# Casts of single heads and half copies for the first batch of an attention and max-out kernel

## Chip, cores and metric

The kernel runs on one core of one Trainium2 chip. The metric is the device time of one execution in microseconds; several executions give a median. A profile of one execution shows every instruction with its engine, line and tile. The engines are TensorE (PE in the profile, its weight loads PEld), VectorE (DVE), ScalarE (ACT), GpSimd (POOL) and SyncE (SP, which here only issues transfers).

## What is computed

Attention over 4 batches, 8 heads, 768 positions of 64 numbers, followed by a max-out layer. Heads marked in `is_retrieval` (three of eight) attend to all earlier positions, the others to a window of 64 and the first 4 positions:

```python
scores = scale * np.matmul(q, k.transpose(0, 1, 3, 2))
stream_keep = causal & (is_sink | in_win)
mask = np.where(retr[0, :, 0, 0, None, None], full_mask, stream_mask)
scores = np.where(mask[None, :, :, :], scores, -1000000000.0)
a = np.exp(scores - max) / sum
x = (a @ v), heads side by side: 3072 rows of 512
h1 = x @ w1          # 512 -> 1024
h2 = x @ w2
out = np.maximum(h1, h2) @ w_out     # 1024 -> 512
```

(The softmax and the reshaping are shortened here.)

## The kernel before

Everything is computed on TensorE in bfloat16. The max-out is rewritten: with wd = w1 - w2 and wm = w2 @ w_out, the result is relu(x @ wd) @ w_out + x @ wm. So, before the dense layers, w1 and w2 are subtracted (L442), w2 is cast, turned on TensorE (L453) and copied, and multiplied with w_out (L464).

Heads are taken in pairs, four pairs in a batch, sixteen in all (`pair`, L659). The heads are permuted so that the three that attend to everything come first: pair 0 of a batch has two such heads, pair 1 one, pairs 2 and 3 none. For each pair, q, k and v are loaded head by head into buffers `ld` (nine of them, three for a pair), cast to bfloat16 into `qb` (L681 to L685), turned by six 128x128 transposes into one bank of PSUM (L690 to L695), and copied from there to `qk` (L696). One bank holds the 768 bfloat16 columns of q or of k, and the copy rearranges them. For batch 0 the first half of the positions of v comes with three transfers at the start; only the late half is loaded by pair.

`attend` (L522) then computes scores into PSUM (L579), in batch 0 adds the mask by matmuls with an identity (L587), takes the exponential on ScalarE (L600), multiplies with v (L624) and divides by the sums on VectorE (L640, L643). When a batch's four pairs are done its result is turned (L739) and goes through the dense layers (L757, L781, L788), which run among the attention of the next batches.

No engine's order is written by hand. Each piece of work is an `Op` with a cost for every engine that may do it, the operations and buffers that it needs, and a priority. `Plan.schedule` (L74) is a list scheduler: over and over it takes, for each engine, the operation that can start first by its own model (of those that can start at once, the one of lowest priority), and of these the one with the earliest start, then the earliest end. The order that comes out is the order in which instructions are issued on each engine, which works through its queue in that order. Plan time 0 lies near 4.2 us of the trace, where the first planned matmul starts. Waits between engines are put in by the framework.

Points of the model that matter here. Transfers are served one after the other, each at its own rate (L140), from a first moment set by `DMA_FIRST` and `EARLY` (L78). SP takes the startable transfer of lowest priority: the loads of pair r have r, r + 0.01 and r + 0.02 for q, k and v, and the twelve quarters of the weights have the priorities of `LATER` (L176). One quarter of w_out is loaded ahead of the plan (`EARLY`) and is taken as landed at a fixed planned time (L433). VectorE and GpSimd take turns at a port for operations marked `shared` (L114 to L117): one may not start while the other's is under way. `warm` (L417) runs 42 matmuls on TensorE at the start.

Of the kernel before, what the change touches and what calls it, by code (L numbers as in the profile page):

```python
# [10 lines left out]
BF16 = mybir.dt.bfloat16  # L11
I32 = mybir.dt.int32
ALU = mybir.AluOpType
ACT = mybir.ActivationFunctionType
# [156 lines left out]
DMA_FIRST = -2.2  # L171
# [1 line left out]
WIDE_PAIRS = (1, 1, 1, 1, 1, 1, 1, 1, 1, 0, 0, 0, 0, 0, 0, 0)  # L173
X_XBAR = (0, 1, 1, 1)
EARLY = (('wo', 3),)
LATER = {('w2', 0): 3.93, ('w2', 1): 3.55, ('w2', 2): 3.4, ('w2', 3): 3.03, ('w1', 0): 5.86, ('w1', 1): 4.21, ('w1', 2): 6.83, ('w1', 3): 6.11, ('wo', 0): 3.53, ('wo', 1): 1.32, ('wo', 2): 0.84, ('wo', 3): 0.93}  # L176
MASK_TO = 1
NORM = 0.80
PO_TWO = 2
# [1 line left out]
WARM = 4.6  # L181
# [7 lines left out]
def kernel(  # L189
# [19 lines left out]
    nc = tc.nc  # L209
    V = nc.vector  # L210
    B, H, S, D = q.shape
# [28 lines left out]
    ident = tl("ident", [128, 128])  # L240
# [56 lines left out]
    def copy(e, o, i):  # L297
        if e == "ACT":
            nc.scalar.copy(out=o, in_=i)  # L299
        else:  # L300
            issued[e].append((V if e == "DVE" else nc.gpsimd).tensor_copy(out=o, in_=i).ins)  # L301
# [75 lines left out]
    def run(full, head, col, exact):  # L377
        P = Plan(*((SHIFT, HOLD) if exact else ({}, {})))
# [4 lines left out]
        sc_p, po_p, mm_p = map(Pool, map(list, (sc_t, po_t, mm_t) if PO_TWO or not exact else (sc_t, po_t[:1], po_t[1:] + mm_t)))  # L383

        c_m = None
        if exact:
            def f(e):
                V.tensor_sub(out=smk[:, 0:128], in0=causal[:, 0:128], in1=far0[:, 0:128])
                for i in (1, 2, 7, 8, 9):
                    V.tensor_sub(out=smk[:, 128 * i:128 * i + 128], in0=causal[:, 0:128], in1=far[:, 0:128])  # L390
                for i in (3, 4, 5, 6):
                    V.tensor_scalar(out=smk[:, 128 * i:128 * i + 128], in0=far0[:, 128:256], scalar1=-1.0, scalar2=1.0,
                                    op0=ALU.mult, op1=ALU.add)
                for m, o in ((tri, ntri), (smk, nsmk)):
                    V.tensor_scalar(out=o, in0=m, scalar1=1.0, scalar2=-NEG, op0=ALU.subtract, op1=ALU.mult)
            c_m = P.op(f, {"DVE": 2.6}, prio=-20)
        else:
            d_ir = P.op(lambda e: nc.sync.dma_start(out=ir, in_=ir_ap.rearrange("p (h t) -> p h t", t=2)),
                        {"SP": 0.5}, prio=-20, size=0.008, rate=0.3)

            def f(e):
                V.tensor_scalar(out=irn, in0=ir, scalar1=0.0, scalar2=float(H), op0=ALU.not_equal, op1=ALU.mult)
                V.tensor_tensor(out=flag, in0=irn[:, :, 0], in1=irn[:, :, 1], op=ALU.max)
                V.tensor_scalar(out=nsf, in0=flag, scalar1=1.0 / H, scalar2=-1.0, op0=ALU.mult, op1=ALU.add)
                V.tensor_scalar_mul(out=bias_j, in0=nsf, scalar1=-NEG)
                V.tensor_scalar_mul(out=bias_0, in0=bias_j, scalar1=nsink)
                for s in range(H):
                    for m in range(2):
                        V.scalar_tensor_tensor(
                            out=msk[:, s, m, :], in0=(far0 if m == 0 else far), scalar=nsf[:, s:s + 1],  # L410
                            in1=causal, op0=ALU.mult, op1=ALU.add)
            c_m = P.op(f, {"DVE": 5.0}, [d_ir], prio=-20)

        if exact:
            bk = Buf(mm_p)

            def warm(e, bk=bk):  # L417
                for _ in range(int(WARM / 0.107)):
                    nc.tensor.matmul(bk.t[:, 0, 0:128], lhsT=ident, rhs=ident, start=True, stop=True)
            P.op(warm, {"PE": WARM}, (), [bk], prio=-100)  # L420
        d_w = {}
        for name in ("w2", "w1", "wo"):
            for c in range(4):
                if (name, c) in EARLY:
                    P.number += 1
                else:
                    d_w[name, c] = P.op(lambda e, name=name, c=c: load_weight(name, c), {"SP": 0.5},
                                        prio=LATER[name, c], size=0.524, rate=0.35)

        def landed(*keys):  # L430

            return dict(deps=[d_w[k] for k in keys if k in d_w],
                        ready=max([0.0] + [DMA_FIRST + 6.05 + 1.7 * EARLY.index(k) for k in keys if k in EARLY]))  # L433
        wd_ops, w2_ops, wo_ops, wm_ops, w2t_ops = [], [], [], [], []
        for c in range(4):
            w2_ops.append(P.op(lambda e, c=c: copy(e, w2_bf[(slice(None),) + quarter(c)], w_raw[1][(slice(None),) + quarter(c)]),
# [10 lines left out]
        for fch in range(FC):  # L447
            bk = Buf(mm_p)
# [6 lines left out]
            o = P.op(tr, {"PE": 0.23}, w2_ops[2 * (fch // 4):2 * (fch // 4) + 2], [bk], prio=300 + fch)  # L455
            w2t_ops.append(P.op(lambda e, fch=fch, bk=bk: copy(e, w2t[:, fch, :], bk.t[:, 0].bitcast(BF16)[:, 0:d_model]),
                                {"DVE": 0.34, "ACT": 0.5}, [o] + wo_ops, [bk], prio=52 + fch))
        for c in range(KC):
            bk = Buf(mm_p)
# [196 lines left out]
        def tok(t):  # L656
            return t.rearrange("c (p n) -> c p n", n=NB)

        def pair(b, p):  # L659
            r = b * HP + p  # L660
            s0 = 2 * p
            if p == 0:
                xs[b], xt[b], xt_ops[b], norms[b] = Buf(xs_p), Buf(xt_p), [], ([], [])
            raws, loads = [], []
            for i, src in enumerate((q, k, v)):
                t = Buf(ld)
                raws.append(t)
                order, rate = ("(p n)", WIDE) if wide[r] and src is not v else ("(n p)", NARROW)
                two = []
                n0 = NB // 2 if b == 0 and src is v else 0  # L670
                for h in range(2):
                    two.append(P.op(lambda e, t=t, src=src, h=h, order=order, n0=n0: nc.sync.dma_start(
                        out=t.t[:, h, n0:], in_=src[b, bass.ds(head(s0 + h), 1), 128 * n0:].rearrange(
                            f"o {order} d -> p (o n) d", p=128)),
                        {"SP": 0.5}, (), [t], prio=r + 0.01 * i, size=0.0983 if n0 else 0.197, rate=rate))
                loads.append(two)
            qk, vb = Buf(qk_p), Buf(vb_p)
            tk, cast = [], []
            qb = Buf(qb_p)
            for i in range(2):  # L680
                def f(e, i=i):  # L681
                    for h in range(2):
                        copy(e, qb.t[:, i, :, h, :], raws[i].t[:, h])
                cast.append(P.op(f, {"POOL": 0.95, "DVE": 0.75} if b == 0 else {"POOL": 0.95}, loads[i],
                                 [raws[i], qb], prio=r + 0.01 * i, shared=True))  # L685
                if not wide[r]:
                    continue
                bk = Buf(mm_p)

                def tr(e, i=i, bk=bk):  # L690
                    psb = bk.t[:, 0].bitcast(BF16)
                    for n in range(NB):
                        nc.tensor.transpose(psb[:, n * 128:(n + 1) * 128],  # L693
                                            qb.t[:, i, n].rearrange("p h d -> p (h d)"), ident)
                o = P.op(tr, {"PE": 0.34}, [cast[i]], [qb, bk, qk], prio=90 + 2 * r)  # L695
                tk.append(P.op(lambda e, bk=bk, i=i: copy(  # L696
                    e, tok(qk.t[:, i]), bk.t[:, 0].bitcast(BF16)[:, 0:S].rearrange("c (n p) -> c p n", p=128)),
                               {"DVE": 0.90, "ACT": 0.7}, [o], [bk, qk], prio=r))
            if not wide[r]:
                tk.append(P.op(lambda e: nc.sync.dma_start_transpose(  # L700
                    out=qk.t.rearrange("c i (n p) -> c (i n) p", p=128),
                    in_=qb.t.rearrange("p i n h d -> p (i n h d)")),
                    {"SP": XBAR}, cast, [qb, qk], prio=r - 0.5, size=0.393, rate=0.2))
            n0 = NB // 2 if b == 0 else 0
            ov = []
            if b == 0:
                def fh(e):
                    for h in range(2):
                        copy(e, vb.t[:, h, 0:n0, 0:D], v_half[:, bass.ds(head(s0 + h), 1)].rearrange(
                            "p o (n d) -> p (o n) d", d=D))  # L710
                ov.append(P.op(fh, {"POOL": 0.6, "ACT": 0.6}, bufs=[v_held, vb], prio=r + 0.04, ready=DMA_FIRST + 5.2))

            def fv(e):
                for h in range(2):
                    copy(e, vb.t[:, h, n0:, 0:D], raws[2].t[:, h, n0:])
            ov.append(P.op(fv, {"POOL": 0.58, "DVE": 0.48} if b == 0 else {"POOL": 0.95}, loads[2],
                           [raws[2], vb], prio=r + 0.05, shared=True))

            last[0] = attend(b, p, qk, vb, tk, ov, r)
# [111 lines left out]
    with tc.If(match >= 1) as branch:  # L831
        _, at = nc.values_load_multi_w_load_instructions(
            perm[0:1, 0:H], engines=(mybir.EngineType.SP, mybir.EngineType.Pool, mybir.EngineType.Activation), min_val=0, max_val=H - 1,
            skip_runtime_bounds_check_because="a permutation of the heads")
# [45 lines left out]
```

## Time and profile before

| | us |
|---|---|
| median of 9 executions | 187.81 |
| lowest, highest | 186.58, 190.58 |
| the profiled execution | 188.12 |
| its span, first to last instruction | 186.3 |
| PE busy | 172.2 |
| ACT busy | 115.0 |
| DVE busy | 87.9 |
| POOL busy | 49.7 |

The mean granted clock of TensorE in the profiled execution was 0.972 of full speed. Busy times of engines overlap. A matmul's duration in the profile includes its way through the array, so TensorE shown as busy need not be working at its peak. "Idle before" in a row is the time that the engine stood before that instruction, with what ended the wait. A transfer's row on SP is its issue; it lands some microseconds later (a median of 4.8 for a load of q, 6.5 for a quarter of w1 or w2).

### The profile page before, as it was taken

The page shows a single profiled execution, that of the slowest core. Times are in us where ns is not written, and L with a number is a line of the kernel's source. Part 1 is how long each engine was busy: PE and PEld are TensorE (multiplying, and loading weights), DVE is VectorE, ACT ScalarE, POOL GpSimd, SP SyncE. Part 2 cuts the span into 40 slices and gives each one's busy share as a digit, 9 for nine tenths or more (in the row PEclk, how much of TensorE's full clock was granted, in tenths as well). Part 3 has the DMA queues.
Part 4 walks back from the last instruction along what each step waited for, and adds up shares of the span by engine and source line. Part 5 has one row for each costly group of instructions (what it writes and reads, how often), then busy time and mean ns, then how long its engine had stood idle before and what let it go on. Part 6 is the DMA issues. An engine that isn't in the chain of part 4 may idle for free.

```text
span 186.3 us, 4604 instructions
## 1 busy us (share of the span) xinstructions
PE 172.2 (92%) x1663; PEld 101.2 (54%) x1663; DVE 87.9 (47%) x247; ACT 115.0 (62%) x191; POOL 49.7 (27%) x107
## 2 busy tenths in 40 slices
PE   1848989899999999999999999999999999999990
PEld 1825665656666555555565556446555545545460
DVE  5636685868788386544478273354743000000000
ACT  3236699968889678726894478268845624426330
POOL 2101051356995765523125415200000000000000
PEclk9975699999999999999999999999999999999999
DMA  5999999999999998999999999994016612012032
GB/s 117 293 240 349 288 262 341 310 315 327 311 307 234 201 224 201 240 244 172 270 208 252 240 219 194 322 202 174 4 58 177 106 60 113 0 73 96 4 113 70
DMA packets 79553, 36.96 MB, mean 198 GB/s; under 512 B 68642, under 2 KB 73506, under 8 KB 79522
## 3 DMA queue, kind: packets, MB, share of 16 engines
q1 hardware_dynamic: 79522, 36.58, 79.0%
q8 instruction: 15, 0.25, 0.6%
q14 instruction: 16, 0.13, 0.2%
HBM read 25.17 MB, written 6.29 MB: 169 GB/s over the span
## 4 chain that ended last, share of the span: by engine, by line
PE 80%; DMA 8%; SPq 2%; DVE 2%; issue 1%; DVEq 0%; ACT 0%
PE mm L757 12%; PE mm L781 11%; PE po L624 8%; PE sc L579 8%; PE po L757 8%; PE po L781 7%; PE mm L788 6%; DMA raw<-in_moe_w_dram 5%; PE sc L781 4%; PE po L788 3%; DMA ld<-in_q_dram 3%; PE mm L464 3%; PE sc L757 2%; PE sc L788 2%; PE mm L693 2%; SPq L310 1%
## 5 line engine op out<-in xcount | busy, mean ns | idle before, releaser
L600 ACT ACTIVATE at_all<-sc 128x1024 bf16<-128x1024 f32 (+2 forms) x72 | 59.6, 870 | 8.2 <-PE sc L587 4.1
L757 PEld LDWEIGHTS <-wd_bf 128*128 128x128 bf16 x256 | 23.2, 98 | 14.0
L301 POOL CAST qb<-ld 128x384 bf16<-128x384 f32 x50 | 24.1, 507 | 19.5 <-DMA ld<-in_k_dram 8.1
L757 PE MATMUL mm<-xt,wd_bf 128*128 128x384 bf16 x140 | 27.6, 326 | 0.0
L624 PEld LDWEIGHTS <-at_all 128*128 128x128 bf16 x472 | 22.1, 100 | 9.5 <-issue 1.5
L624 PE MATMUL po<-vb,at_all 128*128 128x65 bf16 x472 | 26.8, 198 | 0.1
L579 PE MATMUL sc<-qk 64*128 64x128 bf16 (+2 forms) x364 | 23.6, 243 | 1.8 <-ACT qk L299 0.9
L643 DVE TENSOR_TENSOR xs<-po,rz 128x192 f32 x64 | 22.8, 357 | 3.1 <-DVE rz L640 0.9
L781 PEld LDWEIGHTS <-raw 128*128 128x128 bf16 x152 | 14.1, 98 | 13.6
L579 PEld LDWEIGHTS <-qk 64*128 64x128 bf16 x364 | 12.8, 95 | 14.5 <-issue 9.9
L301 POOL CAST vb<-ld 128x384 bf16<-128x384 f32 (+1 forms) x28 | 12.9, 484 | 24.4 <-DMA ld<-in_v_dram 10.4
L640 DVE RECIPROCAL rz<-po 128x6 f32<-128x6 f32 x32 | 6.2, 193 | 26.6 <-PE po L624 26.5
L757 PE MATMUL po<-xt,wd_bf 128*128 128x384 bf16 x88 | 17.9, 326 | 0.0
L781 PE MATMUL mm<-wo_bf,raw 128*128 128x512 bf16 x64 | 16.1, 379 | 0.0
L611 DVE TENSOR_TENSOR at_all<-at_all,smk 128x1024 bf16<-128x1024 bf16 (+3 forms) x27 | 15.2, 582 | 0.0
L788 PEld LDWEIGHTS <-xt 128*128 128x128 bf16 x100 | 9.3, 97 | 9.3
L611 DVE TENSOR_TENSOR at_all<-at_all,tri 128x256 bf16<-128x256 bf16 (+1 forms) x36 | 9.8, 305 | 6.4 <-ACT at_all L600 6.4
L788 PE MATMUL mm<-wm_bf,xt 128*128 128x512 bf16 x48 | 12.3, 379 | 0.0
L299 ACT COPY ot<-mm 128x512 f32<-128x512 f32 x9 | 5.3, 585 | 11.1 <-PE mm L788 10.6
L765 ACT ACTIVATE raw<-mm 128x384 bf16<-128x384 f32 x20 | 9.8, 490 | 2.9 <-PE mm L757 2.6
L781 PE MATMUL po<-wo_bf,raw 128*128 128x512 bf16 (+1 forms) x48 | 11.3, 361 | 0.0
L299 ACT COPY qk<-mm 128x768 bf16<-128x768 bf16 x9 | 7.3, 807 | 5.0 <-PE mm L693 4.4
(91 smaller groups left out, 189.7 us busy)
## 6 DMA issues: line engine op xcount, KB each, us to landing
ld<-in_q_dram SPq DMA_DIRECT2D x32, 192.0 KB, 4.8
ld<-in_k_dram SPq DMA_DIRECT2D x32, 192.0 KB, 4.6
out_dram<-ot SPq DMA_DIRECT2D x23, 256.0 KB, 2.6
ld<-in_v_dram SPq DMA_DIRECT2D x24, 192.0 KB, 4.1
raw<-in_moe_w_dram SPq DMA_DIRECT2D x8, 512.0 KB, 6.5
raw<-in_moe_w_out_dram SPq DMA_DIRECT2D x4, 512.0 KB, 6.0
xt<-in_v_dram SPq DMA_DIRECT2D x3, 256.0 KB, 3.6
ld<-in_v_dram SPq DMA_DIRECT2D x8, 96.0 KB, 3.9
```

The costliest lines, as they stand in the source:

```text
L299: nc.scalar.copy(out=o, in_=i)
L301: issued[e].append((V if e == "DVE" else nc.gpsimd).tensor_copy(out=o, in_=i).ins)
L579: nc.tensor.matmul(sc.t[:, k, off:off + w], lhsT=qk.t[64 * h:64 * h + 64, 1, j * 128:(j + 1) * 128], rhs=qk.t[64 * h:64 * h + 64, 0, q0:q0 ...
L600: nc.scalar.activation(out=a.t[:, k:k + m, 0:n], in_=sc.t[:, k:k + m, 0:n], func=ACT.Exp, scale=scale, bias=0.0 if bias is None else bias[ ...
L611: issued["DVE"].append(V.tensor_mul(out=y, in0=y, in1=z).ins)
L624: nc.tensor.matmul(po[u].t[:, 0, o:o + D + 1], lhsT=a.t[:, k, off + t * 128:off + (t + 1) * 128], rhs=vb.t[:, h, j, :], **fresh(u))
L640: V.reciprocal(out=rz_, in_=p4[:, :, :, D])
L643: V.tensor_tensor(out=xs[b].t[:, n0:n0 + nn, bass.ds(col(s0 + h), D)], in0=p4[:, i, :, 0:D], in1=rz_[:, i].unsqueeze(2).to_broadcast([128, ...
L757: nc.tensor.matmul(bk.t[:, 0, 0:GT], lhsT=wd_bf[:, c, f * 128:(f + 1) * 128], rhs=xt[b].t[:, g * NB // NG:(g + 1) * NB // NG, c, :], start ...
L765: nc.scalar.activation(out=gt.t[:, f, :], in_=bk.t[:, 0, 0:GT], func=ACT.Relu)
L781: nc.tensor.matmul(bk.t[:, 0, 0:m1 - m0], lhsT=gt.t[:, f, t * 128:(t + 1) * 128], rhs=wo_bf[:, f, m0:m1], start=(f == 0), stop=False)
L788: nc.tensor.matmul(bk.t[:, 0, 0:m1 - m0], lhsT=xt[b].t[:, c0 // 128, c, :], rhs=wm_bf[:, c, m0:m1], start=False, stop=(c == KC - 1))
```

## The change

For batch 0, the cast of q or k of a pair was one step with two instructions, one for each head, given to GpSimd or VectorE as a whole; it becomes two steps of one head each, which wait each for its own load and are placed one by one. The copy of the turned q or k out of PSUM was one step with one instruction on VectorE or ScalarE; for batch 0 it becomes two steps, each of half of the positions, which are placed one by one. With that come new numbers for the planner: other priorities of the weights' quarters, 0.55 in place of 0.5 for the issue of a load, and a planned landing 0.5 later for the early quarter of w_out. The definition of `warm` moves up in the text, in the same branch.

```diff
-LATER = {('w2', 0): 3.93, ('w2', 1): 3.55, ('w2', 2): 3.4, ('w2', 3): 3.03, ('w1', 0): 5.86, ('w1', 1): 4.21, ('w1', 2): 6.83, ('w1', 3): 6.11, ('wo', 0): 3.53, ('wo', 1): 1.32, ('wo', 2): 0.84, ('wo', 3): 0.93}
+LATER = {('w2', 0): 3.98, ('w2', 1): 3.71, ('w2', 2): 3.13, ('w2', 3): 0.06, ('w1', 0): 4.72, ('w1', 1): 5.94, ('w1', 2): 6.68, ('w1', 3): 7.85, ('wo', 0): 1.81, ('wo', 1): 3.16, ('wo', 2): 0.46, ('wo', 3): 1.9}
...
-                        ready=max([0.0] + [DMA_FIRST + 6.05 + 1.7 * EARLY.index(k) for k in keys if k in EARLY]))
+                        ready=max([0.0] + [DMA_FIRST + 6.55 + 1.7 * EARLY.index(k) for k in keys if k in EARLY]))
...
-                        {"SP": 0.5}, (), [t], prio=r + 0.01 * i, size=0.0983 if n0 else 0.197, rate=rate))
+                        {"SP": 0.55}, (), [t], prio=r + 0.01 * i, size=0.0983 if n0 else 0.197, rate=rate))
...
-                def f(e, i=i):
-                    for h in range(2):
-                        copy(e, qb.t[:, i, :, h, :], raws[i].t[:, h])
-                cast.append(P.op(f, {"POOL": 0.95, "DVE": 0.75} if b == 0 else {"POOL": 0.95}, loads[i],
-                                 [raws[i], qb], prio=r + 0.01 * i, shared=True))
+                one_ = []
+                for hs in ((0,), (1,)) if b == 0 else ((0, 1),):
+                    def f(e, i=i, hs=hs):
+                        for h in hs:
+                            copy(e, qb.t[:, i, :, h, :], raws[i].t[:, h])
+                    one_.append(P.op(f, {"POOL": 0.48, "DVE": 0.38} if b == 0 else {"POOL": 0.95},
+                                     [loads[i][h] for h in hs], [raws[i], qb], prio=r + 0.01 * i, shared=True))
+                cast += one_
...
-                o = P.op(tr, {"PE": 0.34}, [cast[i]], [qb, bk, qk], prio=90 + 2 * r)
-                tk.append(P.op(lambda e, bk=bk, i=i: copy(
-                    e, tok(qk.t[:, i]), bk.t[:, 0].bitcast(BF16)[:, 0:S].rearrange("c (n p) -> c p n", p=128)),
-                               {"DVE": 0.90, "ACT": 0.7}, [o], [bk, qk], prio=r))
+                o = P.op(tr, {"PE": 0.34}, one_, [qb, bk, qk], prio=90 + 2 * r)
+                for p0, p1 in ((0, 64), (64, 128)) if b == 0 else ((0, 128),):
+                    w = (p1 - p0) / 128
+                    tk.append(P.op(lambda e, bk=bk, i=i, p0=p0, p1=p1: copy(
+                        e, tok(qk.t[:, i])[:, p0:p1],
+                        bk.t[:, 0].bitcast(BF16)[:, 0:S].rearrange("c (n p) -> c p n", p=128)[:, p0:p1]),
+                                   {"DVE": 0.1 + 0.8 * w, "ACT": 0.1 + 0.65 * w}, [o], [bk, qk], prio=r))
```

## The prediction

> **What bounds the kernel now.** I read the page's engine shares and its 40 slices first, then the chain of waits over 0 to 50 us and over the rest, then the table of windows and the timeline of the first 40 us. The page gives TensorE 92% of the span. The chain says what stands ahead of that:
>
> ```profile
> 10.32 5.95 DMA ld<-in_q_dram
> ...
> 25.05 9.79 DMA raw<-in_moe_w_dram
> ...
> 34.86 0.70 DVE w_bf L301
> ...
> 37.65 0.86 PE mm L464 x4
> ...
> 49.76 0.21 DVE rz L640
> 49.97 0.02 issue
> 49.99 0.37 DVE xs L643
> ```
>
> Columns are start, duration, what. Until 34.8 us the chain goes from transfer to transfer. The last of them is the fourth quarter of w2, whose cast ends at 35.6. From there every step is TensorE's, but for one hole of about 1.05 us (49.74 to 50.79), until the output's tail at 181.6. So the end can move by three things only: when that quarter lands, how much TensorE work of batch 0 is still undone by 37.65, and holes after it. TensorE's own work is not touched: no matmul is added or removed.
>
> The windows by 5 us (span, then busy time and count of PE, PEld, DVE, ACT, POOL, then clock, DMA share, GB/s) show what batch 0 runs against:
>
> ```profile
> 10.00:15.00 5.00, 3.19 (x30) 1.79 (x31) 1.64 (x5) 2.58 (x3) 0.00 (x0) 0.69 0.96 268
> 15.00:20.00 5.00, 4.29 (x39) 2.65 (x39) 3.55 (x7) 3.05 (x4) 0.64 (x2) 0.50 1.09 340
> 20.00:25.00 5.00, 5.00 (x81) 3.81 (x80) 4.05 (x14) 3.58 (x7) 0.58 (x2) 0.79 0.92 236
> 25.00:30.00 5.00, 4.26 (x59) 2.71 (x56) 3.66 (x9) 4.84 (x8) 2.17 (x8) 1.00 0.97 336
> 30.00:35.00 5.00, 4.89 (x76) 3.17 (x72) 3.50 (x9) 4.96 (x8) 0.52 (x2) 1.00 1.01 339
> ```
>
> The DMA engines are full from 10 us on (shares 0.92 to 1.09), so w2's last quarter lands by the sum of the bytes ahead of it. ScalarE is the bound between 25 and 35 (9.80 of 10 us). TensorE runs at half clock in 15 to 20; in windows of 1 us that is so from 12 to 22.
>
> And the start, as the timeline has it:
>
> ```profile
> 11.01 0.36 DVE L301 CAST qb<-ld 128x384 bf16<-128x384 f32 x1 [0.28 <-DMA ld<-in_k_dram]
> 11.41 0.35 DVE L301 CAST vb<-ld 128x192 bf16<-128x192 f32 x1
> ...
> 11.98 0.80 ACT L299 COPY qk<-mm 128x768 bf16<-128x768 bf16 x1 [0.36 <-PE mm L693]
> ...
> 12.68 0.36 DVE L301 CAST vb<-ld 128x192 bf16<-128x192 f32 x1 [0.92 <-DMA ld<-in_v_dram]
> 12.83 0.13 PEld L579 LDWEIGHTS <-qk 64*128 64x128 bf16 x4 [1.06 <-ACT qk L299]
> ```
>
> The first scores wait for ScalarE's copy of k; VectorE is stuck in its queue until 12.68, on a cast of v.
>
> **The casts by single heads.** The instructions stay 16: before, one step issued two, now two steps issue one each. In the trace each cast already waits for its own head's load (the casts at 8.98, 9.85, 10.37, 11.01 are apart), so an earlier start is not won by the split. Whether they change engine I worked out by hand from the planner's rules, for the order only: at each cast of pair 0 VectorE and GpSimd could start at the same planned time (GpSimd may not start before VectorE's turn at the port has ended), and the tie goes to the lower cost, 0.38 against 0.48. So they stay on VectorE and the term is 0. If one goes to GpSimd it costs 0.50 instead of 0.36 (rows of 128x384), 0.14 on the path; if one really ran beside another it would win 0.36. Bounds for the start: -0.36 to +0.28 (q and k).
>
> **The copies in halves.** Eight copies become sixteen. The half (384 columns) is not in the trace as a copy; the nearest rows of that width out of PSUM are ScalarE's 128x384 activation, 0.49, and VectorE's 128x384 operation, 0.55 (L767). So a pair of halves takes 0.55 side by side and 1.04 in turn, against 0.80 on ScalarE alone. For the k of pair 0 neither end decides. By the planner's costs k's transposes are due at 7.46, when the cast of v's late heads (due 7.15, ending 7.63) is already placed on VectorE; ScalarE takes the first half, VectorE the second, behind that cast. In the trace that cast waits for its load until 12.68 and ends at 13.04. The second half then runs 13.05 to 13.60, and the scores start near 13.65 instead of 12.83: **+0.8**, where a clean split would have given 11.98 + 0.55 = 12.53, that is -0.3. I take +0.8, because the order is fixed in the queue and the load's time is not changed. Queued behind the waiting instruction on VectorE are only weight casts (their loads are later), so nobody else waits.
>
> The Trainium skill speaks against running the halves side by side at all: PSUM — Partial Sum Buffer, "PSUM bank collisions raise a hardware error", says that two engines, ScalarE and VectorE both reading included, must not be in one bank of the same partitions at once and are to be guarded by bank. Both halves lie in one bank (768 bf16 are 1,536 bytes). If the program is guarded that way, each pair costs 1.04 plus a semaphore, if not 0.55; no instruction of this trace shows such a pair.
>
> Later, where ScalarE is the bound, the copies of pairs 2 and 3 cost it 4 halves in place of 2 whole ones: 4 x 0.49 - 2 x 0.80 = **+0.36**. Ends: -1.6 (none of the eight halves on ScalarE) and +2.3 (all eight, 8 x 0.49 - 1.60); the planner takes whichever engine is free first, so four is the middle.
>
> **The order of loads.** SP issues by priority (pair r has r to r + 0.02, weights have LATER). Before: pair 0, wo2, pair 1, wo1, pairs 2 and 3, w2.3, w2.2, wo0, w2.1, w2.0, pair 4; the timeline of SP agrees. After: pair 0, w2.3, wo2, pair 1, wo0, pairs 2 and 3, w2.2, wo1, w2.1, w2.0, pair 4. The set ahead of w2.0 is the same, so its landing at 34.8 is costed at 0 (bounds ±0.5, about a tenth of a share over the 5 us from 20, where the engines were at 0.92, and as much the other way). w1's quarters change places among themselves; its last stays ahead of pair 7, whose buffers are not yet free when SP gets there: 0. But pairs 1 and 2 each come one chunk later: 524 KB at (268 + 340)/2 = 304 GB/s is 1.72 us.
>
> For pair 1 that reads: q's second head landed at 16.27 (the chain), its transposes followed at 16.71, ahead of the score of pair 0's fourth tile (17.68), which stood behind them in TensorE's queue. The first exponential of pair 1 came 6.50 after the landing, at 22.77. After: landing 17.99; planned one tile later, the transposes now stand behind that score, whose 0.54 + 0.33 (chain) is done in the wait. 17.99 + 6.50 - 0.87 = 23.62, **+0.85** on pair 1, in which the late start above is contained, since pair 0's tiles have that much room (ScalarE stood 1.56 us before the exponential at 18.65). Ends: +0.35 if the halves run side by side and TensorE is never blocked, +1.72 if the order does not adapt. Pair 2's casts stood ready behind other work (22.57, no wait), so its delay is hidden up to about 1.2 us (22.57 less the landing near 21.4: k's issue at 16.8 and 4.6 to landing); 0.5 is left, behind pair 1's delay: 0.
>
> The gain: w2.3's cast leaves the stretch after 22 us (0.69 on VectorE at 28.42). VectorE is not the bound there (7.2 of 10), ScalarE is, and it has w2.2's cast of 1.04 at 30.34. If the planner now gives that to VectorE, -1.04, else 0. I take half, **-0.52**.
>
> The half clock: TensorE got its full clock back at 22, after working without a hole from 17. If the work that ends there comes 0.85 later, that much more time passes at half speed: 0.5 x 0.85 = **+0.42**; ends 0 and +1.7 (a further third of that 10 us stretch, 3.4 us, at half rate). The skill's TensorE: Matmul & The Clock Gate, Part 1, has the clock decided in free-running windows of about 3.4 us, idle ones halving it; the 10 us at half clock here would be three such windows. By that rule the cost would be either 0 or about 1.7, nothing between.
>
> **Sum.** 0 + 0.36 + 0.85 - 0.52 + 0.42 = +1.11 at the end of batch 0's attention. It doesn't all reach the end: from 37.65 on TensorE has the combined weight's product (8 x 0.86 = 6.9 us) to do meanwhile. What of batch 0 is still open then must be done later. TensorE was busy throughout 20 to 25, so I let 0.9 of it through (ends: none and all): **+1.0**. The profiled execution took 188.12 (span 186.3 and 1.82 around it), 0.31 above the median of 187.81; on it the sum gives 189.1, on the median **188.8**. Own range of this case: 187.9 to 189.8.
>
> About 0.5% (0.94 us) is what a measurement of this kernel can tell from no change.
>
> **Rivals.**
> 1. *Weights earlier win* (0.30). For: w2.3 takes the place of wo2, cast at 15.23, in the queue and can be cast some 13 us earlier than at 28.42; if with that w2.2's cast leaves ScalarE, it ends batch 0 before 35.6, so its matmuls that now stand in the chain behind it (0.35 at 36.49 and 0.19 at 37.46) are gone from there, and the hole of 1.05 at 49.74 is closed by the new order: -1.59, 186.2. Against: the last quarter's landing sets the product's start and has not moved.
> 2. *The clock comes back a step later* (0.15). One mechanism: TensorE waits for pair 1's q and k between 18 and 22 us, the full clock comes at 25.5 instead of 22, and 3.4 us of work take twice as long: +1.7 in place of 0.42, with the rest of the sum let through whole: 1.11 - 0.42 + 1.7 = 2.4, 190.2. It decides from a hole of about 1 us there (before: none).
> 3. *Nothing comes through* (0.13, 187.8). The product at 37.65 and what follows hide all of it, and the casts stay where they were; for it speaks that TensorE is the whole chain from there.
> The forecast itself has 0.42; it lies on the edge of what can be told apart, and 0.30 of its 0.42 above it, because its ends upward are larger.
>
> **Chances.** Slower: 0.30 + 0.15 + 0.02 (of rival 3) = 0.47. Faster: 0.28 (of rival 1) + 0.01 + 0.03 = 0.32. Within: 0.11 + 0.02 + 0.08 = 0.21. The range goes from just below rival 1's time, 185.8, to just above rival 2's, 190.4; about 0.12 and 0.06 lie outside.
>
> **What would show it.** Right: a copy of 128x384 on VectorE starting after the cast of v at about 13.0, the first scores near 13.6, pair 1's first exponential after 23.2, both halves' rows near 0.49 and 0.55, w2.0 landing at 34.8, all casts of pair 0 on VectorE. Wrong: the first scores before 12.6; w2's last cast before 34; the product's start (first L464) earlier than 37; a clock of 1.00 already before 21. The full clock first after 24 would be rival 2.

## The result, and the profile after

| | before | after |
|---|---|---|
| median, us | 188.29 (54 executions) | 190.25 (17) |
| lowest, highest | 186.58, 190.58 | 188.99, 192.24 |
| the profiled execution | 188.12 | 189.86 |
| its span | 186.3 | 187.7 |
| clock over the span | 0.972 | 0.990 |

The ratio is 1.0119 with a 95% interval of 1.0092 to 1.0146; it leaves out the executions of either kernel that ran in a slower state, so it isn't the quotient of the two medians above. That is slower by about 2.2 us (0.0119 x 188.29). The forecast was slower by 1.0. The spans differ by 1.4.

The chain of waits of the changed kernel, the lines that answer to those shown of before (start, duration, what):

```profile
27.05 8.93 DMA raw<-in_moe_w_dram
36.00 0.71 DVE w_bf L301
...
38.87 0.86 PE mm L463 x4
...
51.02 0.21 DVE rz L639
51.25 0.37 DVE xs L642
```

This is the chain of before, one step later throughout: w2's last quarter is issued at 27.05 (25.05 before), it lands at 35.98 (34.83), its cast starts at 36.00 (34.86), the product's matmuls stand in the chain at 38.87 (37.65), and the hole of TensorE comes at 51 in place of 50. By the first row of the product itself, in the chain or not, it starts at 38.71 in place of 37.48. From that row to the end it is 187.7 - 38.71 = 149.0 us, and 186.3 - 37.48 = 148.8 before. So the span's 1.4 us are 1.14 of landing, 0.09 between cast and product, and 0.2 behind it.

The windows of the changed kernel (span, then busy time and count of PE, PEld, DVE, ACT, POOL, then clock, DMA share, GB/s):

```profile
8.00:36.00 28.00, 23.04 (x280) 14.97 (x278) 17.62 (x45) 18.66 (x29) 6.19 (x18) 0.94 0.94 289
...
10.00:15.00 5.00, 3.83 (x30) 2.24 (x31) 2.61 (x7) 1.96 (x3) 0.00 (x0) 1.00 0.90 274
15.00:20.00 5.00, 3.57 (x47) 2.17 (x47) 2.86 (x8) 3.82 (x6) 0.56 (x2) 1.00 0.93 295
20.00:25.00 5.00, 5.00 (x61) 3.43 (x62) 3.95 (x10) 3.29 (x7) 2.18 (x6) 0.66 0.95 279
25.00:30.00 5.00, 4.56 (x58) 2.91 (x56) 3.76 (x12) 4.51 (x8) 2.02 (x6) 1.00 0.87 241
30.00:35.00 5.00, 4.23 (x68) 3.12 (x68) 2.65 (x9) 3.46 (x5) 0.87 (x5) 1.00 1.03 352
```

The long window of the kernel before, for the same stretch:

```profile
8.00:36.00 28.00, 22.91 (x287) 15.12 (x286) 18.57 (x45) 19.83 (x27) 4.30 (x13) 0.82 0.99 302
```

The DMA engines moved 302 GB/s before and 289 after, at a share of 0.99 and 0.94; the gap is widest in 25 to 30 (336 and 241 GB/s). They ran dry more often: the share is 0.87 to 0.95 in the first four of the short windows, where before only 20 to 25 was under 0.96. ScalarE, which I took for the bound of 25 to 35, has room now (7.97 of 10 us, 9.80 before), and the time is longer all the same: it wasn't what set the end.

SP's issues in the changed kernel, with the group's start, duration and what is loaded:

```profile
9.00 0.48 SPq L310 DMA_DIRECT2D raw<-in_moe_w_dram  x1
9.53 0.46 SPq L310 DMA_DIRECT2D raw<-in_moe_w_out_dram  x1
10.18 0.90 SPq L671 DMA_DIRECT2D ld<-in_q_dram  x2
11.26 1.72 SPq L671 DMA_DIRECT2D ld<-in_k_dram  x2
13.17 0.96 SPq L671 DMA_DIRECT2D ld<-in_v_dram  x2
15.87 0.38 SPq L310 DMA_DIRECT2D raw<-in_moe_w_out_dram  x1
...
26.54 0.98 SPq L310 DMA_DIRECT2D raw<-in_moe_w_dram  x2
```

And in the kernel before:

```profile
9.11 0.48 SPq L310 DMA_DIRECT2D raw<-in_moe_w_out_dram  x1
9.79 0.88 SPq L672 DMA_DIRECT2D ld<-in_q_dram  x2
10.85 0.85 SPq L672 DMA_DIRECT2D ld<-in_k_dram  x2
11.89 1.67 SPq L672 DMA_DIRECT2D ld<-in_v_dram  x2
13.61 0.49 SPq L310 DMA_DIRECT2D raw<-in_moe_w_out_dram  x1
...
24.49 1.92 SPq L310 DMA_DIRECT2D raw<-in_moe_w_dram  x2
```

Two quarters (w2.3, that is quarter 3 of w2, and wo2, quarter 2 of w_out) now stand in a row ahead of pair 1, and SP stands longer: in the program every SP transfer waits for the one eight before it. The quarter ahead of pair 2, for one, goes out at 15.87, right after the landing (15.85) of w2.3, which was issued eight transfers earlier; that is 2.26 later than before. From 9 us to the issue of w2's last quarter, SP's waits for weights to land sum to 2.5 us, and to 1.5 before. The same set of issues, from the first of these rows to the issue of w2's last quarter, takes SP 18.05 us (9.00 to 27.05), and 15.94 before (9.11 to 25.05). About half of the difference is these waits; the rest is in single issues that last longer (the second load of k in the row at 18.27 takes 1.33 us, where others of k take 0.33). So the candidate at this point was the order of the weights, not the casts or the copies.

### The profile page after: what moved, and what is told of

The parts are those of the page before. It is cut to its first block, busy times and chain, and to the rows that moved or that the text cites. A ratio compares the mean times of both kernels' runs of the same rounds, so it can differ in the third digit from the quotient of the medians.

```text
span 187.7 us, 4614 instructions
## 1 busy us (share of the span) xinstructions
PE 172.9 (92%) x1663; PEld 101.5 (54%) x1663; DVE 87.5 (47%) x252; ACT 113.7 (61%) x189; POOL 51.5 (27%) x112
## 4 chain that ended last, share of the span: by engine, by line
PE 80%; DMA 8%; SPq 3%; DVE 1%; issue 1%; POOL 0%; ACT 0%; POOLq 0%
PE mm L786 13%; PE mm L762 12%; PE po L623 8%; PE sc L578 8%; PE po L762 8%; PE mm L793 6%; PE po L786 6%; DMA raw<-in_moe_w_dram 5%; PE sc L786 4%; DMA ld<-in_k_dram 4%; PE po L793 3%; PE sc L762 2%; PE sc L793 2%; PE po L463 2%; PE mm L463 2%; SPq L671 2%
## 5 line engine op out<-in xcount | busy, mean ns | idle before, releaser
L301 POOL CAST qb<-ld 128x384 bf16<-128x384 f32 x55 | 26.4, 506 | 35.8 <-DVE at_all L610 17.9
L623 PE MATMUL po<-vb,at_all 128*128 128x65 bf16 x472 | 26.8, 197 | 0.1
L762 PE MATMUL mm<-xt,wd_bf 128*128 128x384 bf16 x140 | 26.7, 326 | 0.0
L786 PE MATMUL mm<-wo_bf,raw 128*128 128x512 bf16 (+1 forms) x80 | 19.2, 368 | 0.0
L762 PE MATMUL po<-xt,wd_bf 128*128 128x384 bf16 x88 | 17.3, 326 | 0.0
L793 PE MATMUL mm<-wm_bf,xt 128*128 128x512 bf16 (+1 forms) x56 | 13.9, 371 | 0.0
L299 ACT COPY ot<-mm 128x512 f32<-128x512 f32 (+1 forms) x11 | 6.2, 566 | 11.1 <-PE mm L793 10.7
L610 DVE TENSOR_TENSOR at_all<-at_all,tri 128x256 bf16<-128x256 bf16 (+1 forms) x36 | 8.8, 277 | 6.7 <-ACT at_all L599 6.6
L301 DVE COPY qk<-mm 128x384 bf16<-128x384 bf16 (+1 forms) x14 | 9.0, 666 | 3.8 <-PE mm L695 2.6
L695 PEld LDWEIGHTS <-qb 128*128 128x128 bf16 x108 | 7.2, 103 | 5.7 <-DVE qb L301 3.7
L695 PE MATMUL mm<-ident,qb 128*128 128x128 bf16 x78 | 7.3, 237 | 3.2 <-DVE qb L301 3.1
```

The source lines that it names most:

```text
L610: issued["DVE"].append(V.tensor_mul(out=y, in0=y, in1=z).ins)
L623: nc.tensor.matmul(po[u].t[:, 0, o:o + D + 1], lhsT=a.t[:, k, off + t * 128:off + (t + 1) * 128], rhs=vb.t[:, h, j, :], **fresh(u))
L695: nc.tensor.transpose(psb[:, n * 128:(n + 1) * 128], qb.t[:, i, n].rearrange("p h d -> p (h d)"), ident)
L762: nc.tensor.matmul(bk.t[:, 0, 0:GT], lhsT=wd_bf[:, c, f * 128:(f + 1) * 128], rhs=xt[b].t[:, g * NB // NG:(g + 1) * NB // NG, c, :], start ...
L786: nc.tensor.matmul(bk.t[:, 0, 0:m1 - m0], lhsT=gt.t[:, f, t * 128:(t + 1) * 128], rhs=wo_bf[:, f, m0:m1], start=(f == 0), stop=False)
L793: nc.tensor.matmul(bk.t[:, 0, 0:m1 - m0], lhsT=xt[b].t[:, c0 // 128, c, :], rhs=wm_bf[:, c, m0:m1], start=False, stop=(c == KC - 1))
```

## The experiments

In every row below, "issue" and "landing" are those of w2's last quarter, "cast" is the start of the last cast of w2, "product" the first matmul of w2 x w_out, all in that kernel's one profiled execution; "share" is the DMA share over 8 to 36 us. A cast can start later than the landing, when its engine is still at other work.

| run | ratio, 95% | span | issue, landing | cast | product | share |
|---|---|---|---|---|---|---|
| before | 1 | 186.3 | 25.05, 34.83 | 34.86 | 37.48 | 0.99 |
| after | 1.0119, 1.0092 to 1.0146 | 187.7 | 27.05, 35.98 | 36.00 | 38.71 | 0.94 |
| e12, before again | one execution, 187.13 | 185.4 | 24.56, 33.40 | 33.59 | 36.50 | 1.02 |
| e11, after again | one execution, 189.75 | 187.6 | 26.75, 35.92 | 35.94 | 38.65 | 0.96 |
| e3, casts alone | 0.9978, 0.9937 to 1.0019 | 185.4 | 24.96, 33.75 | 33.87 | 36.40 | 1.01 |
| e4, halves alone | 1.0014, 0.9979 to 1.0049 | 186.8 | 25.33, 35.02 | 35.04 | 37.91 | 0.99 |
| e2, after with old priorities | 1.0026, 0.9993 to 1.0059 | 186.7 | 24.30, 33.54 | 34.81 | 37.49 | 1.00 |
| e5, after with w2.3 back | 1.0001, 0.9973 to 1.0029 | 187.6 | 23.91, 34.51 | 34.53 | 37.22 | 0.98 |
| e1, new priorities alone | 1.0377, 1.0314 to 1.0439 | 191.4 | 26.22, 34.88 | 35.69 | 39.51 | 0.97 |
| e6, w2.3 early alone | 1.0377, 1.0329 to 1.0426 | 193.1 | 27.34, 35.81 | 36.63 | 40.47 | 0.94 |
| e9, w2.3 behind pair 1 | 1.0291, 1.0243 to 1.0339 | 191.6 | 25.57, 34.70 | 34.72 | 37.99 | 1.00 |
| e10, v of pair 0 between | 1.0042, 1.0006 to 1.0079 | 186.5 | 25.89, 34.33 | 34.98 | 37.68 | 0.98 |
| e13, w2.3 from ScalarE | 1.0055, 1.0017 to 1.0093 | 187.7 | 26.90, 35.83 | 35.85 | 38.57 | 0.95 |
| e14, w2.3 from GpSimd | 1.2812, 1.2727 to 1.2897 | 239.5 | 26.19, 34.31 | 35.86 | 39.11 | 0.97 |
| e7, w2 before pair 3 | 1.0224, 1.0149 to 1.0298 | 190.8 | 20.40, 28.47 | 30.06 | 33.38 | 1.01 |
| e8, w2.0 behind pair 4 | 1.2681, 1.2609 to 1.2753 | 236.6 | 30.80, 37.71 | 37.73 | 46.38 | 1.00 |

**Which part of the change.** e1 gives the kernel before all twelve new priorities and nothing else; e2 gives the changed kernel all the old ones; e3 and e4 make only the casts or only the copies new.

```diff
 e1, against before (e2, against after, is the reverse)
-LATER = {('w2', 0): 3.93, ('w2', 1): 3.55, ('w2', 2): 3.4, ('w2', 3): 3.03, ...
+LATER = {('w2', 0): 3.98, ('w2', 1): 3.71, ('w2', 2): 3.13, ('w2', 3): 0.06, ...
 e3, against before: of the diff above, L681 to L690 only
+                one_ = []
+                for hs in ((0,), (1,)) if b == 0 else ((0, 1),):
 e4, against before: of the diff above, L696 to L698 only
+                for p0, p1 in ((0, 64), (64, 128)) if b == 0 else ((0, 128),):
```

> The kernel before with the changed kernel's twelve priorities of the weights (LATER) and nothing else. Theory A (the order of the transfers: two quarters of weights ahead of pair 1 fill the eight transfers that may be under way, the DMA engines run dry later, the last quarter of w2 lands about 1.2 us later and everything after it with it): the whole loss is here, ratio 1.009 to 1.014, first product matmul (L464) at 38.5 to 39.2 us instead of 37.5. Theory B (the halves go one after the other on their bank and hold VectorE up): ratio 0.998 to 1.004 here. Theory C (casts one by one on GpSimd, slower and in turns with VectorE): the same, 0.998 to 1.004.

> The changed kernel with the twelve old priorities; casts, halves and the planner's other numbers as changed. Theory A: the loss is gone, ratio 0.997 to 1.004, last quarter of w2 landing within 0.4 us of 34.8. Theories B and C: the loss stays, 1.008 or more.

> The kernel before with the casts of batch 0 by single heads and nothing else. Theories A and B: 0.997 to 1.003. Theory C: 1.005 or more, with casts of q or k of batch 0 on GpSimd at 0.50 instead of 0.36.

> The kernel before with the PSUM copies of batch 0 in halves and nothing else. Theory A: 0.997 to 1.004. Theory B: 1.007 or more, with the second half of a bank never starting before the first has ended, on whichever engine.

The casts (0.9978) and the halves (1.0014) are each no change within their intervals, and so is the change without its priorities (1.0026). The priorities alone cost more than the whole change: 1.0377. So the loss is theirs, and there is something more in e1 (over the 1.014 at most that was expected) that the rest of the change keeps away.

**Which priority.** Of the twelve, the one that stands out in SP's issues is w2.3. e5 puts it back in the changed kernel, e6 moves it alone in the kernel before.

```diff
 e5, against after, in LATER
-('w2', 3): 0.06
+('w2', 3): 3.03
 e6, against before, in LATER
-('w2', 3): 3.03
+('w2', 3): 0.06
```

> The changed kernel with one of the twelve priorities undone: the quarter w2.3 goes back from 0.06 to 3.03, behind pair 3; one quarter again stands ahead of pair 1. If the two quarters in a row ahead of pair 1 are the cause: ratio 0.998 to 1.005, DMA share over 8 to 36 us at 0.97 or more, first product matmul at 37.2 to 37.9 us. If another of the new priorities is (w_out's quarters in another order, w1's): ratio stays at 1.008 or more and the product starts after 38.4.

> The kernel before with that one priority changed, w2.3 from 3.03 to 0.06; nothing else. If two quarters in a row ahead of pair 1 starve the DMA engines: share under 0.97, last quarter of w2 cast at 35.6 or later, ratio 1.005 to 1.04. If the loss with all new priorities came from w1's order and what it does to the dense layers later: product start as before and ratio under 1.004.

e5 takes the whole loss away (1.0001), with eleven new priorities, the casts and the halves left in; e6 brings all of e1's by that one number (1.0377). One entry is the cause. The profiled execution of e5 was the longest of its twelve (189.43; the median is 188.41), so its span is no measure of it; its chain shows the earlier landing:

```profile
23.91 10.60 DMA raw<-in_moe_w_dram
34.53 0.70 DVE w_bf L301
...
37.38 0.86 PE mm L463 x4
```

e6 and e1 hold more than the later landing. The chain of e6, from the product on:

```profile
40.47 1.02 PE po L464 x4
...
54.38 0.86 PE mm L464 x4
55.40 0.97 PE mm L464 x4
```

The planner made another order on every engine: the product's last matmuls end at 56.4 us in place of 48.7 before. From the product's start to the end it is 152.6 us (193.1 - 40.47), not 148.8.

**Is it that two quarters stand in a row?** e9 leaves the start alone and puts w2.3 behind pair 1, where it is again in a row with another quarter; e10 keeps w2.3 at the start but lets the late v of pair 0 go between.

```diff
 e9, against before, in LATER
-('w2', 3): 3.03
+('w2', 3): 1.2
 e10, against after, in LATER
-('w2', 3): 0.06
+('w2', 3): 0.015
```

> The kernel before with w2.3 at 1.20, so that two quarters in a row stand between pairs 1 and 2 instead of ahead of pair 1. If it is the row of two that starves the queue of transfers (each later transfer waits for the one eight before it): share under 0.97 and the last quarter of w2 at 35.4 us or later, ratio 1.003 to 1.012. If it is that pair 1 comes late: last quarter at 34.9 or earlier, ratio under 1.003.

> The changed kernel with w2.3 at 0.015: still two quarters ahead of pair 1, but with the two loads of v of pair 0 between them. If the row of two is what starves the queue: about half of the loss is gone, last quarter of w2 at 35.0 to 35.6, ratio 1.002 to 1.008. If the number of quarters ahead of pair 1 decides: as the changed kernel, 36.0 and 1.009 to 1.015.

e9 is a miss for the row as such: share 1.00, cast at 34.72, as before. It is slow all the same (1.0291), for what comes later. Its windows:

```profile
60.00:65.00 5.00, 3.82 (x77) 3.04 (x77) 4.60 (x9) 4.24 (x7) 3.07 (x4) 1.00 1.16 219
65.00:70.00 5.00, 3.42 (x37) 2.00 (x37) 4.70 (x15) 4.16 (x7) 2.60 (x6) 1.00 1.26 219
70.00:75.00 5.00, 4.41 (x44) 2.41 (x41) 2.78 (x8) 2.87 (x6) 4.56 (x11) 1.00 1.09 211
```

TensorE (first figure behind the span) stands for 1.18, 1.58 and 0.59 us there, 3.35 in all, with VectorE at 4.6 to 4.7 of 5 in the first two; in the kernel before and in the changed one it is busy for all of these 15 us. So 3.35 of the 5.3 us by which e9's span is longer are holes in a stretch that the change doesn't touch. e10 gives back most of the loss (1.0042; its interval ends at 1.0079, below the 1.0092 where that of the change begins), about as the row of two had it; its last quarter lands at 34.33.

**Does SP's queue carry it?** e13 and e14 issue w2.3 from another engine's queue, so that it stands in front of nothing on SP. In e13 (ScalarE) it keeps its place among the transfers that wait for the one eight before; in e14 (GpSimd) it has a semaphore of its own.

```diff
 e13 and e14, against after
-        nc.sync.dma_start(out=dst[:, rows, cols],
+        (by or nc.sync).dma_start(out=dst[:, rows, cols],
...
-                    d_w[name, c] = P.op(lambda e, name=name, c=c: load_weight(name, c), {"SP": 0.5},
+                    by_act = exact and (name, c) == ("w2", 3)
+                    d_w[name, c] = P.op(lambda e, name=name, c=c, by_act=by_act: load_weight(name, c, nc.scalar if by_act else nc.sync),
+                                        {"ACT": 0.1} if by_act else {"SP": 0.5},
-                                        prio=LATER[name, c], size=0.524, rate=0.35)
+                                        prio=LATER[name, c], size=0.524, rate=0.35, ready=4.4 if by_act else 0.0)
```

(e14 has nc.gpsimd and "POOL": 1.0 in these places, and one more condition in the rule for turns at the port, for a GpSimd step that comes before any VectorE step.)

> The changed kernel with w2.3's early transfer issued by ScalarE at about the same moment instead of by SP. In the program it keeps its place among the eight semaphores that the transfers take in turn (each transfer waits for the one eight before it). If that rotation is what makes SP late: as the changed kernel, last quarter of w2 cast at 35.4 us or later, ratio 1.006 to 1.014. If SP's own time for one more issue, or its place in SP's queue, is it: 35.2 or earlier and under 1.006.

> The same with GpSimd issuing it: in the program it then has a semaphore of its own outside the eight, and SP's waits are again those of the kernel before. The same bytes stand ahead of pair 1 and ahead of the last quarter. If the rotation is what makes SP late: SP issues w2.0 by 25.6 instead of 27.0, last quarter cast at 35.2 or earlier, ratio under 1.006. If the bytes ahead of pair 1 are what counts: 35.6 or later, 1.007 or more.

The chain of e13, from the issue of the last quarter:

```profile
26.90 8.94 DMA raw<-in_moe_w_dram
35.85 0.70 DVE w_bf L301
```

e13 lands as late as the change (35.83), as its expectation has it if the rotation makes SP late. It doesn't clear SP's queue: w2.3 went out at 7.21, not at 9.00, and came ahead of loads of pair 0 (its v landed at 14.87 and 15.24, at 11.36 and 12.22 in the changed kernel), and SP, free of w2.3 itself, waited 2.8 us (2.0 and 0.8) for loads of k and v of pair 0 and issued the last quarter at 26.90, hardly earlier. What it shows is that sparing SP one issue doesn't bring the landing back. By its ratio e13 is better than the change (1.0055, just short of the 1.006 expected with the rotation; its interval ends at 1.0093 and just meets that of the change), which its one profile doesn't show.

e14 has its last cast late too (35.86), but not its last landing: the last quarter was issued at 26.19 and landed at 34.31, within what the kernels with w2.3 at its old place have, and its cast stood 1.55 us behind other work of VectorE. So e14, with w2.3 outside the rotation, speaks for the rotation rather than against it, and against the bytes ahead of pair 1 as the carrier. It is no proof: the issue at 26.19 is later than the 25.6 that was expected, w2.3 went out at 7.64 here, and the planner's order is another one. e14's time, 1.2812, doesn't come from the landing: TensorE waits from 65 us on and runs at half clock, as in e8 below (clock 0.843 over the span).

**Is the landing a law or a part of one?** e7 (with the casts of e3) brings w2 forward ahead of pair 3; e8 holds w2.0 back behind pair 4.

```diff
 e7, against e3, in LATER
-('w2', 0): 3.93, ('w2', 1): 3.55, ('w2', 2): 3.4, ('w2', 3): 3.03, ('wo', 0): 3.53
+('w2', 0): 2.9, ('w2', 1): 2.8, ('w2', 2): 2.6, ('w2', 3): 2.5, ('wo', 0): 2.7
 e8, against before, in LATER
-('w2', 0): 3.93
+('w2', 0): 4.05
```

> The kernel before with the casts by single heads and the five last quarters of w2 and w_out ahead of pair 3 (priorities 2.50 to 2.90). Pair 3 is 0.98 MB of transfers, 3.2 us. If the landing sets the end: last cast near 31.6, product from 34.2, and an end earlier by what pair 3's own work, now later, leaves over: ratio 0.985 to 1.000. If the planner's order on the engines suffers as it did with the weights early on the kernel before: ratio 1.015 or more, with waits of TensorE for VectorE between 60 and 80 us.

> The kernel before with the last quarter of w2 (w2.0) at 4.05 instead of 3.93, which puts it behind pair 4 and leaves the first 25 us of transfers as they were. Pair 4 is 1.18 MB, at the 302 GB/s of this stretch 3.9 us. If the landing of the last quarter sets the start of the product (L464) and that the end: cast at 38.4 to 39.2, product from 41 to 42, ratio 1.010 to 1.025. If the end follows from elsewhere and TensorE fills the time with pair 4: ratio under 1.006.

Neither came out as the landing alone would have it. e7 lands 6.4 us earlier, casts 4.8 and starts the product 4.1 earlier, and is slower (1.0224): 157.4 us follow its product's start, in place of 148.8. The waits for VectorE between 60 and 80 us that were expected in that case didn't come (TensorE is busy for 19.99 of these 20 us). Between 88 and 94 TensorE stands for 2.95 us, 1.9 of them in one wait for a transposing transfer of the batch's result (xt<-xs), and then it runs at half clock for some 6.8 us; in the kernel before it is busy for all of 80 to 100. The hole and the half of 6.8 us that the clock cost make some 6 of the 8.6 us; why the batch's result came late there stays open. In e8 a shift of one transfer past one pair's loads gave 1.2681. What TensorE waited for in e8 (engine, tile and line, what for, us in total, times, longest):

```profile
PE po L624 <- DVE xs L643: 8.9, 11, 1.1
PE sc L579 <- DMA qk<-qb: 8.0, 4, 3.3
PE po L624 <- DVE at_all L611: 4.5, 4, 1.3
```

None of these three waits is among those of the kernel before. And the clock of e8's later windows:

```profile
70.00:75.00 5.00, 1.96 (x28) 1.57 (x28) 2.66 (x9) 1.45 (x3) 3.69 (x9) 0.59 1.11 214
75.00:80.00 5.00, 2.13 (x36) 1.97 (x37) 0.91 (x3) 0.00 (x0) 1.53 (x4) 0.50 1.26 200
...
80.00:100.00 20.00, 10.90 (x137) 7.83 (x133) 10.13 (x30) 11.01 (x18) 6.80 (x16) 0.50 1.31 211
```

TensorE is busy for less than half of 70 to 80, falls to half clock, and stays there until some 135 us (0.61 over 120 to 140, 1.00 from 140 on).

**The spread of a landing.** e11 and e12 are the two kernels once more, unaltered, side by side.

> The changed kernel once more, for a second look at its profile. If the late landing belongs to the order: last quarter of w2 cast at 35.4 us or later, product from 38.1 or later. If it was this one execution's: near 34.8 and 37.5.

> The kernel before once more, for a second look. If the landing belongs to the order: last quarter cast at 34.3 to 35.2, product from 36.8 to 37.8, end 148.6 to 149.4 us after the product's start.

After repeats: landing at 35.92 (35.98 the first time), cast at 35.94 (36.00). Before comes earlier than expected: landing at 33.40 (34.83), cast at 33.59 (34.86), and 148.9 us from the product to the end, as expected. Taken over all kernels that hold w2.3 at its old place and keep the order behind it (before, e12, e2, e3, e4, e5), SP issues the last quarter at 23.91 to 25.33; with w2.3 at the start (after, e11, e1, e6, e13, e14, e10) at 25.89 to 27.34. These groups don't overlap. The last cast starts at 33.59 to 35.04 and, but for e10 (34.98), at 35.69 to 36.63. The landings lie at 33.40 to 35.02 and at 34.31 to 35.98, and do overlap: e10, e14 and e1 (34.88) land within the first group, and the casts of e1 and e14 are late by work of VectorE.

**What stays open** is how w2.3 at the start makes the last landing late. Shown is that SP issues the last quarter later whenever w2.3 stands there. Not shown is what holds SP. The row as such isn't enough (e9), and to spare SP one issue doesn't help (e13). The wait for the eighth transfer before fits e13 and e14, but in e10 SP waits 1.9 us for w2.3 as well, and the last quarter lands at 34.33. "A megabyte ahead of pair 1" fits neither e10 nor e14, which both have it. But each of these is one profile, and two executions of the kernel before landed 1.43 us apart. No version was found that is clearly faster than the kernel before; the nearest, e3, has an interval that holds 1.

## Why the prediction was right and wrong

**Right: the bound.** The last quarter of w2 and then TensorE set the end. Product's start plus 148.8 to 149.2 us gives the span in nine profiles: before, after, e2, e3, e4, e10, e11, e12, e13. The four kernels with another order behind it (e1, e6, e9, e7) have 151.9 to 157.4, and e5's one execution 150.4; e8 and e14, with their long stretch at half clock, have 190 and 200.

**Wrong: the step "The set ahead of w2.0 is the same, so its landing at 34.8 is costed at 0 (bounds ±0.5 ...)".** It measured +1.15 in the profile and +2.52 between e12 and e11 (landing), and it reached the end (spans +1.4 and +2.2). The sum of bytes was the same; the moment at which SP issued the last quarter was not (27.05 in place of 25.05), nor the rate. The step rests on two readings in the prediction's first part, that "Until 34.8 us the chain goes from transfer to transfer" and that the DMA engines are full, "so w2's last quarter lands by the sum of the bytes ahead of it". The chain of the kernel before doesn't go so. Between the landing of pair 1's q and the last quarters it goes through 6.4 us of casts, matmuls and divisions, and then through SP's queue:

```profile
16.29 0.37 DVE qb L301
...
22.05 0.61 DVE wo_bf L301
22.67 0.22 SPq L672
```

The quarters of w2 are issued behind loads of pair 3 that wait for VectorE, and pair 1 itself lands later after the change, as the prediction had it. So the issue of the last quarter could move although the bytes ahead of it were the same. In the sum this was nothing; it is the result. That the sum of the other terms came to +1.0, slower as measured, is luck: they are not what made it slower.

**Wrong in place: the lateness of batch 0.** Pair 1's first exponential came at 23.32, +0.55 (forecast +0.85, low end +0.35). But e2 to e5 and the relation above leave little for it to add: between last cast and product 2.71 us passed after, 2.62 before. Of the 0.9 that I let through, 0.1 shows ahead of the product.

**The casts, right.** The four of pair 0 stayed on VectorE (9.38, 9.90, 10.43, 11.00). From pair 1 on some went to GpSimd (first at 19.44, 0.51 us); e3 says that this is worth nothing measurable.

**The halves: prices right, the start wrong.** The timeline of the changed kernel's start:

```profile
11.17 0.48 ACT L299 COPY qk<-mm 128x384 bf16<-128x384 bf16 x1 [2.56 <-PE mm L695]
11.68 0.56 DVE L301 COPY qk<-mm 128x384 bf16<-128x384 bf16 x1 [0.32 <-ACT qk L299]
12.16 0.60 DVE L301 CAST vb<-ld 128x192 bf16<-128x192 f32 x2
12.28 0.48 ACT L299 COPY qk<-mm 128x384 bf16<-128x384 bf16 x1 [0.63 <-PE mm L695]
12.79 0.56 DVE L301 COPY qk<-mm 128x384 bf16<-128x384 bf16 x1
...
12.81 0.61 PE L578 MATMUL sc<-qk 64*128 64x384 bf16 x4 [0.57 <-ACT qk L299]
```

0.48 on ScalarE and 0.56 on VectorE, where 0.49 and 0.55 were worked out from neighbouring rows. And they run in turn: VectorE's half of q stands for ScalarE's ("0.32 <-ACT qk"), and k's starts 0.03 after the other ends. So a pair costs 1.04 where the whole copy took 0.80. That is what the Trainium skill, PSUM — Partial Sum Buffer, "PSUM bank collisions raise a hardware error", makes one expect: two engines are to be kept out of one bank at once. What I had wrong is the +0.8: the cast of v didn't hold VectorE (12.16, no wait), and the first scores need the first half alone, so they began at 12.81, as before (12.83).

**ScalarE's terms, wrong and without effect.** Two of the eight halves of pairs 2 and 3 went to ScalarE, not four (0.99 us in place of 1.67 for the two whole copies before, so -0.68, not +0.36), and it got two casts of w2, not fewer (31.52 and 34.63, 1.05 each). Neither was on the path.

**The clock, wrong in sign.** TensorE was at half clock from 12 to 22 us before and for some 3 us after 20 in the changed kernel (0.66 in 20 to 25); forecast was a longer stretch. From the share in the windows of 8 to 36, 2 x 28 x (1 - clock) us were at half clock: 10.1 before (0.82), 3.4 after (0.94), 6.7 in e7 (0.88), 0 in e13 (1.00). The skill's TensorE: Matmul & The Clock Gate, Part 1, has the clock decided in free-running windows of about 3.4 us; these are three, one, two and none of that length. The time doesn't follow them: e13 with none has a span of 187.7, e12 with three (0.82 too) one of 185.4, which fits a stretch that ends with a landing anyway.

**The rivals.** "Weights earlier win" named what spoke against it, that the landing had not moved; it did move, the other way. "The clock comes back a step later" fell. "Nothing comes through" is what the change is without w2.3's priority (e5).

## What to carry to other kernels

Where the chain runs through transfers, an order of loads that leaves the same bytes ahead isn't free: look for windows in which the DMA share is under 1, and follow the chain back past the issue of the transfer that counts, before costing it at nothing. Where a list scheduler makes the order, change one number at a time and both ways, since a priority brings its own cost and a new order of everything behind it: the same entry cost 1.2% inside the change and 3.8% alone. And an earlier landing is a gain only if the time from it to the end stays what it was (e7: landing 6.4 us earlier, 2% slower).

## What was not expected of the hardware

With the same set of transfers ahead, the last of them was issued 2.0 to 2.2 us later and landed 1.2 to 2.5 us later (after and e11 against before and e12), with a DMA share of 0.94 to 0.96 in place of 0.99 to 1.02.

Half clock can last. In e8 and e14 TensorE got into waits from 65 us on. About 73 us of e8's span were at half clock (2 x 0.155 x 236.6), some 7 of them before 36 us, the rest in one stretch from some 71 to some 135 us: at 0.50, busy for 10.90 of 20 us in 80 to 100. e9, which stood for 3.35 us in three windows, kept its full clock and lost 2.9%; e8 lost 26.8%. Whether the half clock itself keeps TensorE waiting, or the planner's order does, no run here shows.
